# Linear attention before a GELU MLP on one core: 64-token blocks on 64x64 tiles, and groups of one chunk of each sequence

## The chip, the core and the metric

The kernel runs on one NeuronCore of a Trainium2 chip. Five engines work on their own queues, each strictly in the order of its instructions: TensorE (PE, matrix products, its weight loads shown as PEld), VectorE (DVE), ScalarE (ACT), GpSimd (POOL, which here also issues the loads) and SyncE (SP, which issues stores and transposing DMAs). They meet through semaphores. The metric is the device time of one execution in microseconds (us); lower is better.

## What is computed

Inputs q, k, v are 4 sequences x 8 heads x 768 tokens x 64 values; `lam` has one decay per head. Attention is causal and linear, with a decay of `lam` per token, and its result of 3072 tokens x 512 values goes through an MLP of width 2048 with an exact GELU. The reference, cut to what matters:

```python
for b in range(nb):                       # blocks of 64 tokens
    intra = einsum('bhic,bhjc->bhij', qb, kb) * Dmask     # lam ** (i - j), i >= j
    intra = einsum('bhij,bhjd->bhid', intra, vb)
    inter = einsum('bhid,bhde->bhie', qb * lam_pow, kv_state)
    out[:, :, sl] = intra + inter
    kv_state = lam_block * kv_state + einsum('bhsd,bhse->bhde', kb_dec, vb)
x = out as [B * S, H * D]
y = gelu(x @ w_in) @ w_out
```

The state is carried from block to block within a sequence, and sequences do not depend on each other.

## The kernel before, in words

Matrix operands are bf16, sums and results float32. The work is cut into 24 chunks of 128 tokens, numbered through sequence after sequence (six to a sequence), and into six groups of four consecutive chunks (`M = 4`). A group is 512 tokens, the width of one MLP pass. While PE runs the MLP of one group, the attention of the next is placed between the MLP's blocks.

The MLP of a group (`mlp_blocks`, L276) has 32 blocks: 16 of the first product (`mm1`, four matmuls of 512 columns, L288, then a GELU by ACT, L290) and 16 of the second (`mm2`, four matmuls of 512 columns, L300; after four blocks ACT copies the sum, L305, and SP stores it, L306).

The attention of a chunk has these steps:
- Loads of q, k and v, issued by POOL (L65), three or so chunks ahead (`prefetch`).
- `decay_k` (L157, L167): k times a decay per token, on POOL.
- Transposes of k and of q. The first eight chunks do it on PE (L174) with a copy by ACT (L180) and a product by DVE (L183, `qT`). From chunk 8 on, SP issues transposing DMAs (L189, L191), with `q_hat`, the scaled q, made by POOL in between (L190).
- `scores` (L193): eight matmuls on 64 rows x 128 columns (L198), each 128 columns long, into two banks of `sc`; DVE multiplies them by the mask (L202).
- `next_state` (L204): from chunk 4 on `next_state_full`, four matmuls over two heads each (L238), of which DVE keeps the diagonal blocks by a product with `lam_blk` (L245, L246). The first four chunks do it with eight matmuls of 64 columns on 128x64 tiles (L213). The last chunk of a sequence has no state to make.
- `outputs` (L249): the old state times q (L253, four matmuls; in the first four chunks L259, on 64x64 tiles; none in the first chunk of a sequence) and the masked scores times v (L263, eight matmuls on 128x64 tiles) into the one bank `o`. ACT (first eight chunks, L271) or DVE (L273) copies the result into x, transposed as the MLP wants it.

PE's order is written out by hand. Chunks 0 to 3 run ahead of the MLP (L371 to L396), with idle matmuls (`keep_warm`) between them. Chunks 4 to 7 are placed by the table `group0` into the MLP of group 0. From chunk 8 on, each step has a due time as a share of a group's MLP (`todo`, L438): transposes a third of a group ahead, scores and state of the i-th chunk at 0.06 + 0.245 i, its outputs at the time of the next chunk's scores. Steps that fall due together run in the order outputs, scores, state. PSUM has eight banks: two each for `mh`, `mo` and `sc`, one each for `o` and `t`.

Of the kernel before, what the change touches and what calls it, by code (L numbers as in the profile page):

```python
# [15 lines left out]
def kernel(  # L16
# [14 lines left out]
    C = 128  # L31
    NB = S // C
    NCH = B * NB
# [3 lines left out]
    assert NK1 == HP  # L37


    M = 4  # L40
    NG = NCH // M
    assert NG * M == NCH and M == 4 and NB == 6

# [4 lines left out]
    qkv_pool = ctx.enter_context(tc.tile_pool(name="qkv", bufs=8))  # L48
    work_pool = ctx.enter_context(tc.tile_pool(name="work", bufs=3))
# [4 lines left out]


# [3 lines left out]
    def chunk_of(name, n):  # L59
        b, so = n // NB, n % NB  # L60
        return dram[name][b, :, so * C:(so + 1) * C, :].rearrange("h si d -> si h d")

    def load(n, name):
        raw[n, name] = qkv_pool.tile([128, H, D], BF16, tag=name, name=f"{name}_t")
        nc.gpsimd.dma_start(raw[n, name], chunk_of(name, n))  # L65


    lam_b = consts.tile([128, H], F32)
    nc.sync.dma_start(lam_b, lam[None, :].to_broadcast((128, H)))

    pos = consts.tile([128, 1], F32)
    row = consts.tile([128, C], F32)
    nc.gpsimd.iota(pos, pattern=[[0, 1]], base=0, channel_multiplier=1, allow_small_or_imprecise_dtypes=True)
    nc.gpsimd.iota(row, pattern=[[1, C]], base=0, channel_multiplier=0, allow_small_or_imprecise_dtypes=True)

    for item in "k0 q0 v0 k1 q1 k2 q2 v1 k3 q3 v2 v3".split():
        load(int(item[1]), item[0])

    w_in_t = w_pool.tile([128, NK1, d_ff], BF16)
    w_out_t = w_pool.tile([128, NK2, d_model], BF16)  # L80
    w_in_r = moe_w_in.rearrange("(ko ki) f -> ki ko f", ki=128)
    w_out_r = moe_w_out.rearrange("(ko ki) f -> ki ko f", ki=128)
    NS = 4

    def load_w_in(s):
        f = d_ff // NS
        nc.gpsimd.dma_start(w_in_t[:, :, s * f:(s + 1) * f], w_in_r[:, :, s * f:(s + 1) * f])

    def load_w_out(s):
        f = NK2 // NS  # L90
        nc.gpsimd.dma_start(w_out_t[:, s * f:(s + 1) * f, :], w_out_r[:, s * f:(s + 1) * f, :])
# [4 lines left out]
    cmask = consts.tile([128, C], F32)  # L96
    negj = consts.tile([128, 1], F32)
    cmj = consts.tile([128, 1], F32)
    warm = consts.tile([128, 1], F32)
    nc.vector.tensor_scalar(ident, row, pos, None, op0=ALU.is_equal)  # L100
    nc.vector.tensor_scalar(cmask, row, pos, None, op0=ALU.is_ge)
    nc.vector.tensor_scalar(negj, pos, -1.0, None, op0=ALU.mult)
    nc.vector.tensor_scalar(cmj, pos, -1.0, float(C), op0=ALU.mult, op1=ALU.add)

    lam_blk = consts.tile([128, HP, 128], F32)
    first_blk = consts.tile([128, HP, 128], BF16)
    nc.vector.memset(lam_blk, 0.0)
    nc.vector.memset(first_blk, 0.0)


    ln = consts.tile([128, H], F32)
    ln_col = consts.tile([128, HP], F32)
# [3 lines left out]
    lam_k = consts.tile([128, H], F32)  # L116
    lam_c = consts.tile([128, HP], F32)
    dmask = consts.tile([128, H, C], F32)
    nc.scalar.activation(ln, lam_b, ACT.Ln)
    ln_r = ln.rearrange("p (hp hi) -> p hp hi", hi=2)  # L120
    for hi in range(2):
        p = slice(hi * D, (hi + 1) * D)
        nc.vector.tensor_copy(ln_col[p, :, None], ln_r[p, :, hi:hi + 1])
    nc.scalar.activation(lam_m, ln, ACT.Exp, scale=negj)
    for hp in range(HP):
        nc.scalar.activation(lam_q[:, hp, :], row, ACT.Exp, scale=ln_col[:, hp:hp + 1])
    nc.scalar.activation(lam_k, ln, ACT.Exp, scale=cmj)
    nc.scalar.activation(lam_c, ln_col, ACT.Exp, scale=float(C))
    nc.scalar.activation(lam_p, ln, ACT.Exp, scale=pos)
    lam_c_b = lam_c[:, :, None].to_broadcast((128, HP, D))  # L130

    def make_lam_blk():
        for hi in range(2):
            p = slice(hi * D, (hi + 1) * D)
            nc.vector.tensor_copy(lam_blk[p, :, p], lam_c_b[p])

    def make_dmask():
        nc.vector.tensor_mul(dmask, cmask[:, None, :].to_broadcast((128, H, C)),
                             lam_m[:, :, None].to_broadcast((128, H, C)))


# [3 lines left out]
    xT = {}  # L145
    states = {}

    def bank(shape, dtype, tag, name):
        return ps.tile(shape, dtype, tag=tag, name=name, bufs=2 if tag in ("sc", "mh", "mo") else 1)

    def begin(n, early=False):
        c = Chunk()
        c.n, c.sb, c.early = n, n % NB, early
        c.q, c.k, c.v = (raw.pop((n, name)) for name in "qkv")
        return c

    def decay_k(c, eng):  # L157

        if c.sb == NB - 1:
            return  # L160
        c.k_dec = work_pool.tile([128, H, D], BF16, tag="kd", name="k_dec")
        if eng is nc.scalar:
            for h in range(H):
                nc.scalar.activation(c.k_dec[:, h, :], c.k[:, h, :], ACT.Copy, scale=lam_k[:, h:h + 1])
        else:
            scale = lam_k if c.early else lam_m
            eng.tensor_mul(c.k_dec, c.k, scale[:, :, None].to_broadcast((128, H, D)))  # L167

    def transposes(c, between=lambda: None):

        t_ps = [bank([128, HP, C], BF16, tag, "t_ps") for tag in ("mh", "mo" if c.early else "mh")]
        for dst, src in zip(t_ps, (c.k, c.q)):
            for hp in range(HP):
                nc.tensor.transpose(dst[:, hp, :], src[:, 2 * hp:2 * hp + 2, :], ident)  # L174
            if src is c.k:
                between()
        c.kT = work_pool.tile([128, HP, C], BF16, tag="kT", name="kT")
        c.qT = work_pool.tile([128, HP, C], BF16, tag="qT", name="qT")
        if c.n > 0:
            nc.scalar.copy(c.kT, t_ps[0])  # L180
        else:
            nc.vector.tensor_copy(c.kT, t_ps[0])
        nc.vector.tensor_mul(c.qT, t_ps[1], lam_q)  # L183

    def dma_transposes(c):
        c.kT = work_pool.tile([128, HP, C], BF16, tag="kT", name="kT")
        c.qT = work_pool.tile([128, HP, C], BF16, tag="qT", name="qT")
# [5 lines left out]
    def scores(c):  # L193
        sc_ps = [bank([128, HP, C], F32, "sc", f"sc_ps{hi}") for hi in range(2)]
        for hp in range(HP):
            for hi in range(2):
                p = slice(hi * D, (hi + 1) * D)
                nc.tensor.matmul(sc_ps[hi][:, hp, :], c.kT[p, hp, :], c.qT[p, hp, :], start=True, stop=True)  # L198
        c.sc_m = work_pool.tile([128, HP, 2, C], BF16, tag="sc_m", name="sc_m")
        dmask_r = dmask.rearrange("p (hp hi) i -> p hp hi i", hi=2)  # L200
        for hi in range(2):
            nc.vector.tensor_mul(c.sc_m[:, :, hi, :], sc_ps[hi], dmask_r[:, :, hi, :])  # L202

    def next_state(c):  # L204
        if c.sb == NB - 1:
            return
        if not c.early:
            return next_state_full(c)
        kv_ps = bank([128, HP, D], F32, "t", "kv_ps")
        for hp in range(HP):  # L210
            for hi in range(2):
                h = 2 * hp + hi
                nc.tensor.matmul(kv_ps[hi * D:(hi + 1) * D, hp, :], c.k_dec[:, h, :], c.v[:, h, :],  # L213
                                 start=True, stop=True)
        if c.n == M - 1:
            for hi in range(2):
                p = slice(hi * D, (hi + 1) * D)
                nc.vector.tensor_add(first_blk[p, :, p], kv_ps[p], states[c.n][1][p])
            states[c.n + 1] = first_blk, None
            return  # L220
        new = work_pool.tile([128, HP, D], BF16, tag="state", name="state")
        if c.sb == 0:
            nc.vector.tensor_copy(new, kv_ps)
        else:
            nc.vector.tensor_add(new, kv_ps, states[c.n][1])
        old = work_pool.tile([128, HP, D], F32, tag="old", name="old")
        states[c.n + 1] = new, old

    def decay_state(c):
        new, old = states[c.n + 1]  # L230
        for hp in range(HP):
            nc.scalar.activation(old[:, hp, :], new[:, hp, :], ACT.Copy, scale=lam_c[:, hp:hp + 1])

    def next_state_full(c):

        kv_ps = bank([128, HP, 128], F32, "t", "kv_ps")
        for hp in range(HP):
            nc.tensor.matmul(kv_ps[:, hp, :], c.k_dec[:, 2 * hp:2 * hp + 2, :], c.v[:, 2 * hp:2 * hp + 2, :],  # L238
                             start=True, stop=True)
        new = work_pool.tile([128, HP, 128], BF16, tag="state_f", name="state")  # L240
        if c.sb == 0:
            nc.vector.tensor_mul(new, kv_ps, lam_blk)
        else:
            tmp = work_pool.tile([128, HP, 128], F32, tag="tmp", name="tmp")
            nc.vector.tensor_add(tmp, kv_ps, states[c.n][0])  # L245
            nc.vector.tensor_mul(new, tmp, lam_blk)  # L246
        states[c.n + 1] = new, None

    def outputs(c, x_t, off, evacuate=True):  # L249
# [16 lines left out]
        if evacuate:  # L266
            empty_outputs(c)
# [131 lines left out]
    for s in range(1, NS):  # L399
        load_w_in(s)  # L400
# [104 lines left out]
```

## Time and profile before

| what | us |
|---|---|
| median of three runs (lowest, highest) | 218.54 (217.63, 219.41) |
| span of the profiled execution, first to last instruction | 217.5 |
| median less that span | 1.04 |
| first MLP matmul starts | 19.37 |
| first matmul of the second product starts | 33.55 |
| MLP of group 1 starts | 54.05 |
| last copy of a result starts (chain) | 214.06 |

The profile comes from one execution. Of that execution the span is what is known; the runs' times were taken on their own, and the table sets their median beside it. A group of the profile is a line of the kernel, an engine, an operation and its tiles (out<-in), with the number of instructions, their busy time and the mean duration of one. A matmul's duration holds the way through the array; matmuls follow each other faster than that, so the pace is read from starts. A tile such as 64*128 is rows x columns of the array. The chain of work that ended last goes back from the last instruction to whatever released it.

Loads of q, k or v take POOL 0.88 to 0.92 us each to issue and, in the first 50 us, land 0.9 us apart; a quarter of w_in or w_out takes about 2.5 us more.

### The profile page before, as it was taken

The numbers are of one execution on the slowest core, as the hardware profiler recorded it, in microseconds if no ns is written. First come the engines' busy times: TensorE is split into PE (matmuls) and PEld (weight loads), VectorE is DVE, ScalarE is ACT, GpSimd is POOL, SyncE is SP. The second block draws the span as 40 slices with busy tenths as digits, with TensorE's granted clock in tenths as the row PEclk, the third lists the DMA queues.
The fourth block names the chain that finished last, engine by engine and source line by source line (L and its number), as shares of the span: only waits on it lengthen the run. The fifth ranks groups of instructions, "written<-read, shape, count | busy, mean of one in ns | idle before, by whom it ended". The sixth has DMA issues, their size and how long they took to land.

```text
span 217.5 us, 3545 instructions
## 1 busy us (share of the span) xinstructions
PE 204.9 (94%) x1422; PEld 102.9 (47%) x1446; DVE 74.8 (34%) x120; ACT 91.1 (42%) x169; POOL 105.8 (49%) x120
## 2 busy tenths in 40 slices
PE   7679999999987999999999999999999999999993
PEld 2355444555443544444545444544445545444452
DVE  5884000478516243316225323315415323100000
ACT  6975772434563321365221375221465221566121
POOL 8998333998999999276950809113000000000000
PEclk9999999999999999999999999999999999999998
DMA  5999999999999999999999497515251012100112
GB/s 37 149 169 203 198 194 183 156 208 148 177 150 126 164 128 138 215 110 104 109 114 160 77 180 62 37 48 146 74 98 24 3 57 88 50 0 3 48 49 96
DMA packets 100272, 24.35 MB, mean 112 GB/s; under 512 B 92960, under 2 KB 97312, under 8 KB 100256
## 3 DMA queue, kind: packets, MB, share of 16 engines
q0 software_dynamic: 79104, 13.64, 84.4%
q1 hardware_dynamic: 21152, 10.50, 22.7%
q8 instruction: 11, 0.18, 0.3%
q14 instruction: 5, 0.04, 0.1%
HBM read 27.27 MB, written 6.29 MB: 154 GB/s over the span
## 4 chain that ended last, share of the span: by engine, by line
PE 73%; DMA 14%; POOL 9%; issue 2%; ACT 0%; POOLq 0%
PE o_ps L300 33%; PE h_ps L288 28%; DMA q_t<-in_q_dram 8%; DMA qT<-q_hat 3%; DMA w_in_t<-in_moe_w_in_dram 3%; PE o_ps L263 3%; PE sc_ps L198 3%; POOL k_t L65 3%; POOL q_t L65 2%; POOL v_t L65 2%; PE kv_ps L238 2%; PE o_ps L315 2%; PE o_ps L253 2%; POOL k_dec L167 1%; POOL q_hat L190 1%
## 5 line engine op out<-in xcount | busy, mean ns | idle before, releaser
L288 PE MATMUL h_ps<-x_t,w_in_t 128*128 128x512 bf16 (+2 forms) x378 | 84.8, 377 | 1.0 <-DMA w_in_t<-in_moe_w_in_dram 0.5
L300 PE MATMUL o_ps<-w_out_t,g_t 128*128 128x512 bf16 x355 | 81.8, 379 | 0.8 <-issue 0.3
L290 ACT ACTIVATE g_t<-h_ps 128x512 bf16<-128x512 f32 x96 | 57.3, 597 | 35.3 <-PE h_ps L288 35.3
L288 PEld LDWEIGHTS <-w_in_t 128*128 128x128 bf16 x388 | 37.3, 98 | 43.8 <-DMA w_in_t<-in_moe_w_in_dram 0.6
L300 PEld LDWEIGHTS <-g_t 128*128 128x128 bf16 x368 | 34.7, 98 | 39.6
L305 ACT COPY o_sb<-o_ps 128x512 f32<-128x512 f32 x23 | 13.5, 586 | 68.3 <-PE o_ps L300 62.5
L202 DVE TENSOR_TENSOR sc_m<-sc_ps,dmask 128x512 bf16<-128x512 f32 x48 | 30.8, 683 | 16.1 <-PE sc_ps L198 15.8
L273 DVE CAST x_t<-o_ps 128x512 bf16<-128x512 f32 x16 | 11.1, 692 | 71.4 <-PE o_ps L263 71.4
L190 POOL TENSOR_TENSOR q_hat<-q_t,lam_p 128x512 bf16<-128x512 bf16 x16 | 16.9, 1056 | 20.0 <-DMA qT<-q_hat 19.0
L167 POOL TENSOR_TENSOR k_dec<-k_t,lam_m 128x512 bf16<-128x512 bf16 x16 | 17.7, 1106 | 14.0 <-PE kv_ps L238 8.1
L65 POOL DMA_DIRECT2D k_t<-in_k_dram x24 | 22.1, 920 | 4.0 <-DMA w_out_t<-in_moe_w_out_dram 2.1
L65 POOL DMA_DIRECT2D q_t<-in_q_dram x24 | 21.5, 897 | 4.2 <-DMA w_out_t<-in_moe_w_out_dram 3.4
L65 POOL DMA_DIRECT2D v_t<-in_v_dram x24 | 21.4, 894 | 3.4 <-DMA w_out_t<-in_moe_w_out_dram 1.7
L198 PE MATMUL sc_ps<-qT,kT 64*128 64x128 bf16 x192 | 9.5, 218 | 3.8 <-DMA qT<-q_hat 2.6
L246 DVE TENSOR_TENSOR state<-tmp,lam_blk 128x512 bf16<-128x512 f32 x13 | 12.1, 932 | 0.5
L183 DVE TENSOR_TENSOR qT<-t_ps,lam_q 128x512 bf16<-128x512 bf16 x8 | 5.5, 689 | 18.9 <-PE t_ps L174 18.7
L263 PE MATMUL o_ps<-sc_m,v_t 128*64 128x128 bf16 x192 | 10.1, 225 | 0.0
L198 PEld LDWEIGHTS <-kT 64*128 64x128 bf16 x192 | 5.7, 94 | 8.3 <-issue 4.7
L361 PE MATMUL idle_ps<-idle 128*128 128x512 bf16 x21 | 7.5, 473 | 1.2 <-DVE idle L94 1.2
L245 DVE TENSOR_TENSOR tmp<-kv_ps,state 128x512 f32<-128x512 f32 x12 | 8.2, 681 | 0.0
L180 ACT COPY kT<-t_ps 128x512 bf16<-128x512 bf16 x7 | 4.1, 579 | 9.4 <-PE t_ps L174 9.4
L263 PEld LDWEIGHTS <-v_t 128*64 128x64 bf16 x192 | 6.2, 109 | 3.3 <-issue 0.8
(57 smaller groups left out, 82.7 us busy)
## 6 DMA issues: line engine op xcount, KB each, us to landing
out_dram<-o_sb SPq DMA_DIRECT2D x23, 256.0 KB, 2.6
k_t<-in_k_dram POOLq DMA_DIRECT2D x24, 128.0 KB, 4.6
q_t<-in_q_dram POOLq DMA_DIRECT2D x24, 128.0 KB, 5.9
v_t<-in_v_dram POOLq DMA_DIRECT2D x24, 128.0 KB, 5.9
w_in_t<-in_moe_w_in_dram POOLq DMA_DIRECT2D x4, 512.0 KB, 7.9
w_out_t<-in_moe_w_out_dram POOLq DMA_DIRECT2D x4, 512.0 KB, 15.1
kT<-k_t SPq DMA_TRANSPOSE x16, 4.7
qT<-q_hat SPq DMA_TRANSPOSE x16, 4.0
```

The costliest lines, as they stand in the source:

```text
L65: nc.gpsimd.dma_start(raw[n, name], chunk_of(name, n))
L167: eng.tensor_mul(c.k_dec, c.k, scale[:, :, None].to_broadcast((128, H, D)))
L190: nc.gpsimd.tensor_mul(q_hat, c.q, lam_p[:, :, None].to_broadcast((128, H, D)))
L198: nc.tensor.matmul(sc_ps[hi][:, hp, :], c.kT[p, hp, :], c.qT[p, hp, :], start=True, stop=True)
L202: nc.vector.tensor_mul(c.sc_m[:, :, hi, :], sc_ps[hi], dmask_r[:, :, hi, :])
L246: nc.vector.tensor_mul(new, tmp, lam_blk)
L263: nc.tensor.matmul(o_ps[hi * D:(hi + 1) * D, hp, :], c.v[:, 2 * hp + hi, :], c.sc_m[:, hp, hi, :], start=(c.sb == 0 and hp == 0), stop=Tru ...
L273: nc.vector.tensor_copy(c.x_o, c.o_ps)
L288: nc.tensor.matmul(h_ps[:, lo:hi], w_in_t[:, ki, kf * 128:(kf + 1) * 128], x_t[:, ki, lo:hi], start=(ki == 0 and lo == 0), stop=(ki == NK1 ...
L290: nc.scalar.activation(g_t[:, kf, :], h_ps, ACT.Gelu)
L300: nc.tensor.matmul(om[io], g_t[:, kf, io * C:(io + 1) * C], w_out_t[:, kf, :], start=(kf == 0), stop=(kf == NK2 - 1))
L305: nc.scalar.copy(o_sb, om[io])
```

## The change

Groups are now one chunk of each of the four sequences, so the first group has no old state, and group g holds chunk g of every sequence. The result rows of a block are `io * S + g * C`.

Within a chunk, attention works in blocks of 64 tokens. All its matmuls from chunk 4 on are 64x64 tiles with 64 columns. Rows 0 to 63 of the array hold one head of a pair and rows 64 to 127 the other. Scores and states go to the columns of the same half, outputs to the other half (`half(1 - hi)`; w_in's rows are loaded swapped to match). `visit(f, d)` issues the outputs of chunk f and the scores and states of chunk d in turn, a pair of each. For this, v is loaded by block and head (`load_v`, four DMAs a group), k is copied into the same order (`by_block`, four copies, on ACT for chunks 4 to 7 and on DVE later), and v is decayed by POOL instead of k (`decay_v`). The state between the two blocks of a chunk is `mid`, copied by ACT except in the last group.

The first MLP pass starts with three chunks only: its first 10 blocks take 384 columns, and `rest` takes the fourth chunk's 128 columns later. Group 1 does so with its first 6 blocks. Chunk 3's attention, the first states and the table `dmask` come between MLP blocks. Placing is by block number: visits at blocks 3, 10, 17, 24 and 30 of a group, transposes (`prepare`) at 0, 7, 14 and 21; group 1 has its own list, moved by 2. The raw pools have ten buffers of q and k, the work pool four.

```diff
+    BANKS = dict(mh=2, mo=2, sc=2, o=1, kv=1)
+    def load_v(g):
+        t = raw[g] = qkv_pool.tile([128, 2, B * HP, D], BF16, tag="vg", name="vg_t", bufs=3)
+        src = v.rearrange("b (hp hi) s d -> hi s (b hp) d", hi=2)
+        for u in range(2):
+            for hi in range(2):
+                s = g * C + u * L
+                nc.gpsimd.dma_start(t[half(hi), u], src[hi, s:s + L])
+    for hi in range(2):
+        nc.sync.dma_start(lam_h[half(hi)], lam_pair[hi:hi + 1, :].to_broadcast((64, HP)))
     nc.sync.dma_start(lam_b, lam[None, :].to_broadcast((128, H)))
...
+    def load_w_in(lo, hi_):
+        f = slice(lo * 128, hi_ * 128)
+        for hi in range(2):
+            nc.gpsimd.dma_start(w_in_t[half(1 - hi), :, f], w_in_r[hi, :, :, f])
+    for n in range(3):
+        for name in "kqv":
+            load(n, name)
+    load_w_in(0, 2)
+    load_w_in(2, 5)
+    load_w_in(5, 8)
+    for name in "kqv":
+        load(3, name)
+    load_w_in(8, 12)
+    load_w_in(12, 16)
+    for s in range(4):
+        load_w_out(4 * s, 4 * s + 4)
...
+    def by_block(c, eng):
+        c.k2 = work_pool.tile([128, 2, HP, D], BF16, tag="k2", name="k2")
+        k_r = c.k.rearrange("p (hp hi) d -> p hp hi d", hi=2)
+        for hi in range(2):
+            for u in range(2):
+                if eng is nc.scalar:
+                    nc.scalar.copy(c.k2[half(hi), u], k_r[half(u), :, hi, :])
+                else:
+                    eng.tensor_copy(c.k2[half(hi), u], k_r[half(u), :, hi, :])
+    def decay_v(n):
+        vd[n] = work_pool.tile([128, 2, HP, D], BF16, tag="vd", name="vd", bufs=6)
+        nc.gpsimd.tensor_mul(vd[n], v_of(n), lam_vb)
     def scores(c):
+        sc = c.sc = bank([128, 2, HP, L], F32, "sc", "sc_ps")
+        return [[(sc[half(hi), u, hp, :], c.kT[half(hi), hp, u * L:(u + 1) * L],
+                  c.qT[half(hi), hp, u * L:(u + 1) * L], True) for hi in range(2)]
+                for u in range(2) for hp in range(HP)]
+    def states(c):
+        kv = c.kv = bank([128, 2, HP, D], F32, "kv", "kv_ps")
+        us = range(2) if c.g < NG - 1 else range(1)
+        return [[(kv[half(hi), u, hp, :], c.k2[half(hi), u, hp, :], vd[c.n][half(hi), u, hp, :], True)
+                 for hi in range(2)] for u in us for hp in range(HP)]
+    def next_states(c):
...
+        if c.g == NG - 1:
+            nc.vector.tensor_add(c.mid, c.kv[:, 0], s0)
+            return
+        nc.vector.tensor_add(t1, c.kv[:, 0], s0)
+        nc.scalar.copy(c.mid, t1)
+        nc.vector.tensor_add(t2, c.kv[:, 1], t1)
...
+        nc.vector.tensor_mul(new, t2, lam_cb)
+    def outputs(c):
...
+        for u, s in enumerate((state[c.n], c.mid)):
+            for hp in range(HP):
+                pairs.append([(o[half(1 - hi), hp, u * L:(u + 1) * L], s[half(hi), hp, :],
+                               c.qT[half(hi), hp, u * L:(u + 1) * L], False) for hi in range(2)])
+        for u in range(2):
+            for hp in range(HP):
+                pairs.append([(o[half(1 - hi), hp, u * L:(u + 1) * L], c.v[half(hi), u, hp, :],
+                               c.sm[half(hi), u, hp, :], False) for hi in range(2)])
...
+    def visit(f, d, emptier=None):
...
+        if d:
+            kv = states(d)
+            lists.append(scores(d) + kv)
+        if f:
+            lists.append(outputs(f))
+        issue(*lists)
+        if f:
+            empty(f, emptier or nc.vector)
+        if d:
+            mask(d)
+            next_states(d)
...
+    def prepare(n):
+        c = begin(n)
+        dma_transposes(c)
+        decay_v(n)
+        by_block(c, nc.vector)
+        prefetch(n + B)
+    prefetch(2 * B - 1)
+    for n in range(B, 2 * B):
+        decay_v(n)
+    prefetch(2 * B + 1)
+    ahead = {
+        5: [lambda: pe_transposes(begin(3), ("mo", "mo"))],
+        6: [lambda: scores0(3)],
+        8: [lambda: outputs0(3, nc.scalar)],
+        9: [make_dmask, lambda: decay_k0(0, nc.vector)],
...
+        first: [first_states],
+        first + 8: [group1(4)],
+        first + 11: [lambda: visit(None, 4)],
+        first + 12: [group1(5)],
+        first + 13: [lambda: visit(4, 5, nc.scalar)],
+        first + 14: [group1(6)],
+        first + 15: [lambda: visit(5, 6, nc.scalar)],
+    }
...
+    visit(6, None, nc.scalar)
+    plans = {1: (2, 8, 9, 14, 15, 20, 21, 26, 27, 31)}
+        if g == 1:
+            ahead[1] += [group1(7)]
+            ahead[3] += [lambda: visit(None, 7)]
+            ahead[5] += [lambda: visit(7, None, nc.vector)]
...
+            p = plans.get(g, (None, 3, 0, 10, 7, 17, 14, 24, 21, 30))
```

`first` is 19, the block after the first product of group 0. `scores0`, `outputs0` and `first_states` do the four chunks of group 0, which need no old state, with tiles of 128 tokens as before. `group1(n)` is the PE transposition of a chunk with `by_block` on ACT. `issue` walks through its lists and takes one pair of each in turn.

## The prediction

> **What bounds the kernel now.** I read the page's busy shares first, then the slices of the span, then the chain of work that ended last, and then the timelines of single engines around one attention visit.
>
> ```profile
> PE 204.9 (94%) x1422; PEld 102.9 (47%) x1446; DVE 74.8 (34%) x120; ACT 91.1 (42%) x169; POOL 105.8 (49%) x120
> ...
> DMA  5999999999999999999999497515251012100112
> ...
> PE 73%; DMA 14%; POOL 9%; issue 2%; ACT 0%; POOLq 0%
> ```
>
> TensorE (PE) is busy for 94% of the span, and from 66.57 us on the chain runs on it alone; the DMA engines are full over the first 22 of 40 slices. So PE decides, except where a load or a transpose is late. The MLP is 768 matmuls of 512 columns at 0.216 us, about 166 us, and the change leaves it. What can shrink is the attention between its blocks and the stretch ahead of them. The chain, in order of time (start, length, what), prices one attention visit; the PE timeline shows small tiles:
>
> ```profile
> 106.53 0.22 PE o_ps L253 x4
> 106.75 0.34 PE o_ps L263 x8
> 107.10 0.33 PE sc_ps L198 x8
> 107.43 0.33 PE kv_ps L238 x4
> ```
>
> ```profile
> 15.19 0.32 PE L213 MATMUL kv_ps<-v_t,k_dec 128*64 128x64 bf16 x8
> ...
> 18.04 0.41 PE L259 MATMUL o_ps<-qT,state 64*64 64x128 bf16 x8
> ```
>
> A full visit costs 1.22 us. Of that, L253 runs at 0.055 us a matmul of 128 columns; L263 and L198 take 0.34 and 0.33 for four pairs at about 0.056, so each holds about 0.1 us for the switch between tile shapes, and so does L238. L213 puts eight 64-column matmuls into 0.32 us though one lasts 0.20: their starts spread over 0.12 us, a pair per 0.03 us, two column tiles at a time. L259 is the one 64x64 row: eight matmuls of 128 columns in 0.41 with 0.216 for one, so a pair per 0.055 to 0.06, two tiles at a time on the diagonal. Four tiles at a time occur nowhere.
>
> **Steady visits (chunks 8 to 23).** Before: 16 x 1.22, less three without a state (0.33 each) and two without an old state (0.22 each), 18.1 us; the four places where the chain shows 0.97 for four MLP matmuls instead of 0.86 add 0.4: 18.5. After: 64 matmuls of 64 columns, 32 pairs, of which a diagonal pair (scores, states) stands beside an off-diagonal one (outputs). If four tiles run at once, 16 steps of 0.03, 0.46 us, plus 0.19 for the switch in and out: 0.65. The first and the last visit of a group have 16 pairs alone: 0.65 too. Five visits in each of four groups: 13.0. Gain 5.5. The bounds: pairs strictly in turn make a full visit 1.12, all matmuls singly 2.05. I take four at once, since L213 shows two streams down one set of rows, L198 two row tiles writing the same partitions of two banks, and a step needs nothing else.
>
> Two rules of the Trainium skill speak against it. TensorE: Matmul & The Clock Gate ("Wait — 56ns, not 53.3ns?") has starts never closer than about 25 ns; L213's are closer, but only sixteen instructions long. By that rule an estimate for a full visit is 64 x 25 ns, 1.6 us, and the whole some 20 us slower. TensorEngine Tiling (Array Packing), "Gotcha 1: PSUM Pressure", says that row tiles cannot use one PSUM bank at the same time; L259's two row tiles share o_ps and still pair. By that rule the visit would be the 1.12 case.
>
> **Chunks 4 to 7.** Before, from the chain between 39.17 and 53: transposes 4 x 0.45, scores 4 x 0.33, states 0.77, old states 3 x 0.22, outputs 4 x 0.34, and 0.3 of switches: 6.2. After: the same transposes, 1.8, and six visits of 0.65: 5.7. Gain 0.5.
>
> **Start.** Loads land 0.9 us apart from 6.65 on. Before, h_ps starts at 19.37, behind twelve loads and a quarter of w_in. After, nine loads end near 13.3 and the first slice of w_in (half a quarter; a quarter takes 2.5 us) near 14.6. Chunk 2's queries land near 12.4; then qT 0.69, scores 0.33, two masks 1.3, outputs 0.34, ACT copy 0.59 bring h_ps to about 16.1. The two extra lam loads on SP (0.39 us of issue, as lam_b) delay tables by 0.8, which the DVE's queue absorbs to 0.3. But chunk 3 (1.1 us with switches) and the first states (2 x 0.24 and switches, 0.65) now lie behind 16.1, its queries land near 20.1 (0.5 wait), and w_in's fourth piece near 23.5 (0.2 wait). The second product starts at 16.1 + 13.9 + 1.1 + 0.65 + 0.9 = 32.7, against 33.55. Gain 0.9; bounds 2 and -0.5.
>
> **Waits the change adds around chunks 4 to 7.** Each of by_block's four ACT copies is 64x256; nearest rows are L319 (128x256, 0.37) and L164 (128x64, 0.25 apart), so 0.41 each. After a transposition at t, kT is copied from t+0.47 (as 42.44 to 42.91), the copies end at t+2.65, and the visit one block later wants its first state at t+1.65. PE is in order, so the rest of the visit and the next MLP block queue behind it: 0.9 each for chunks 5 and 6. Chunk 4 waits for vd on POOL: vg's four loads land near 42.2, decay_v takes 1.1, PE comes near 43: 0.3. The next group's first block needs chunk 6's x, an ACT copy (0.59 and its start) with no block between: 0.7. Chunk 7's transposes share mh with the first product: 0.7. A late mid: 0.1. Together 3.6, against 0.2 of small gaps before: loss 3.4. Bounds 0 and 5.
>
> **A wait on ACT.** mid is copied by ACT, in its queue ahead of the next gelu. These rows show the order and pace:
>
> ```profile
> 99.08 0.69 DVE L273 CAST x_t<-o_ps 128x512 bf16<-128x512 f32 x1 [5.77 <-PE o_ps L263]
> 99.68 1.28 DVE L202 TENSOR_TENSOR sc_m<-sc_ps,dmask 128x512 bf16<-128x512 f32 x2
> ```
>
> ```profile
> 98.66 0.60 ACT L290 ACTIVATE g_t<-h_ps 128x512 bf16<-128x512 f32 x1 [0.27 <-PE h_ps L288]
> 100.52 0.60 ACT L290 ACTIVATE g_t<-h_ps 128x512 bf16<-128x512 f32 x1 [1.27 <-PE h_ps L288]
> ```
>
> A gelu starts 1.06 us after its block (99.46 to 100.52) and ends at 1.66; PE wants that bank back at 1.73. After the change: DVE starts 0.18 into the block, x 0.60, mask 0.60, t1 0.41 (L225), ACT 0.05 and 0.40: gelu starts at 2.24, 1.1 too late for PE two blocks on. Without x (a group's first visit) 0.5. Visits at blocks 3 and 10 lie in the first product in groups 2 and 3 (chunks of the last group copy mid on DVE), and one half visit in group 1: 2 x 1.6 + 0.5 = 3.7 lost. Visits in the second product have no gelu behind them. Bounds 0 (ACT idles 0.27 a block) and 5.
>
> **POOL and the transposes.** The kernel before already waits for qT, as the list of waits has it:
>
> ```profile
> PE sc_ps L198 <- DMA qT<-q_hat: 2.6, 2, 2.2
> ```
>
> POOL is busy almost without a break from 38 to 86. The ten w_in loads instead of four cost it 6 x 0.8 more, in the stretch from 20 to 38 where it sat idle 11 us in all before L65, waiting for landings; vg's four loads have as many short rows as four of v. After: four decay_v end near 46.5, eight loads at 0.88 near 53.5, q_hat and decay_v of chunk 8 near 55.6, then ten loads (prefetch to 12, with vg of group 3) to 64.8, and only then q_hat of chunk 9, which ends near 65.9. Its transposition lands 4.0 later (median), 6.9 at worst, near 70; PE comes near 68.6. Wait 1.5 instead of 2.6: gain 1.1; bounds 2.6 gain and 3 loss. SP has only its finished stores ahead. Later chunks have two loads between them and 12 blocks of time.
>
> **Costed at nothing.** DVE's by_block, four copies of at most 0.29 (L135) a chunk: DVE is busy 11.5 of 33 us a group, and the next visit is ten blocks off. Without that cover, 1.2 us a chunk. (An SBUF operation of DVE, L246, stretches from 0.69 to 1.83 while POOL works; even so it fits.) decay_v replaces k_dec at the same 1.1. The split first products reload 64 weight tiles: at 0.003 each beyond the columns, 0.2 lost.
>
> **Sum:** -5.5 - 0.5 - 0.9 + 3.4 + 3.7 - 1.1 + 0.2 = -0.7. The profiled execution spans 217.5; that becomes 216.8. The median of the three runs, 218.54, is 1.04 above that span, which I add for what lies around it: 217.8.
>
> **Rivals.**
> Pairs in turn. For it: no row with four tiles at once, and 128 PE instructions in 0.46 us, twice the density of L213. Against: nothing in L213, L198 or L259 collides. Fourteen full visits take 0.46 longer each, the last three 0.12 less than that: +6.1, 223.9. It decides from 0.2 us a visit on (14 x 0.2 = 2.8 us, over 1%).
> Waits smaller. If ACT's wait and half of those around chunks 4 to 7 are hidden (gelu's bank free earlier, copies shorter), 217.8 - 3.7 - 1.7 = 212.4. For it: DVE and ACT are idle half the time. Against: both queues are in order, and PE's slack is 0.07.
> Transposes late. If q_hat of chunk 9 lands behind ten loads as 59.67 did (6.9 us) and the next two follow suit: +4, 221.8. For it: DMA is full until 114. Against: old chunk 9 had the same and lost 2.2.
>
> **How the numbers follow.** One per cent is about what a measurement can tell: 216.4 to 220.7. Forecast 0.42, own range 215.5 to 220.5 (faster 0.09, same 0.30, slower 0.03). Pairs in turn 0.20, slower. Waits smaller 0.25, faster. Transposes late 0.13, slower 0.11, same 0.02. So faster 0.34, same 0.32, slower 0.34. The range for 8 in 10 reaches into the cases on both sides: 212.4 to 223.9.
>
> **What would show it.** Matmuls of a full visit within about 0.5 us, or 0.9 and more; idle PE of about 1 us two blocks after the visits at blocks 3 and 10 of groups 2 and 3, released by gelu, with ACT's gelu behind mid; PE waiting for the ACT copies of k2 around 45 to 52; the first h_ps near 16; one wait for qT near 69. If a visit takes over 0.85 us, or PE waits elsewhere by more than 3 us, the forecast is wrong.

## The result and the profile after

The changed kernel takes 232.99 us, median of 4 runs (232.14 to 233.70), against 218.73 for the kernel before on the same chip: ratio 1.0666, 95% interval 1.0615 to 1.0716. It is slower by 14.3 us, outside the range of 212.4 to 223.9. The profiled execution spans 231.1 us and took 232.84 by its own time. The time lies about 1.75 us above the span in this and the experiments' runs, where the prediction had added 1.04. Executions more than 1.5% above the fastest of their kernel are left out of what follows unless the text says so: two of four of the kernel without the two loads (230.3 and 231.9), four of eight of the one with whole rows (221.2 to 221.7, not profiled), three single ones of later kernels (720.5, 1157.2 and 219.9), and some of the kernel before.

The page of the changed kernel, in the order in which the lines of before were read:

```profile
PE 203.9 (88%) x2250; PEld 104.1 (45%) x2279; DVE 98.2 (42%) x189; ACT 97.5 (42%) x187; POOL 109.1 (47%) x128
...
PEclk9679999999999999889999999999999999999999
DMA  0999999998999999999999325103234011200112
...
PE 69%; DMA 13%; POOL 6%; ACT 4%; issue 2%; DVE 2%; SPq 1%; POOLq 0%; ACTq 0%
```

PE is busy 1.0 us less than before (204.9), in a span 13.6 us longer: nearly everything that was lost is idle PE. The first of 40 slices of the DMA line has fallen from 5 to 0, and PEclk, before at 9 up to its last slice, shows two dips, in slices 2 and 3 and in slices 17 and 18. DVE, SP's queue and, with more than 0%, ACT have entered the chain.

To place the loss, the starts of each group's MLP are read from PE's timeline (us):

| stretch | before | after | after less before |
|---|---|---|---|
| start to the second product of group 0 | 33.55 | 41.06 | +7.5 |
| from there to the MLP of group 1 | 20.5 | 20.8 | +0.3 |
| group 1 | 35.1 | 41.6 | +6.5 |
| group 2 | 32.4 | 32.65 | +0.25 |
| group 3 | 32.2 | 32.65 | +0.45 |
| group 4 | 32.4 | 31.2 | -1.2 |
| group 5 to the end of the span | 31.3 | 31.1 | -0.2 |

Two stretches hold all of it. What PE waited for (engine, tile and line, releaser: total us, times, longest), from the list of PE's waits after; it covers the whole span, and its row with `g_t` L346 belongs to groups 2 and 3:

```profile
PE t_ps L187 <- DMA k_t<-in_k_dram: 5.9, 1, 5.9
PE sc_ps L279 <- DMA qT<-q_hat: 4.1, 2, 3.4
PE h_ps L344 <- ACT x_t L269: 2.1, 3, 0.8
PE h_ps L344 <- ACT g_t L346: 2.0, 2, 1.0
...
PE h_ps L354 <- DVE x_t L271: 0.9, 1, 0.9
PE sc_ps L279 <- ACT k L209: 0.8, 1, 0.8
```

**The start.** The DMA part of the profile, for the first 12 us alone (40 slices of 0.3 us; under it the packets of SP's queue, and issues with their number, size and median us to landing), of the kernel before and then of the changed one:

```profile
DMA  0000000000249996899999999999999999999999
q1 hardware_dynamic: 144, 0.00, 0.5%
k_t<-in_k_dram POOLq DMA_DIRECT2D x4, 128.0 KB, 4.4
```

```profile
DMA  0000000000000000000000039996999999999999
q1 hardware_dynamic: 688, 0.01, 3.1%
k_t<-in_k_dram POOLq DMA_DIRECT2D x3, 128.0 KB, 9.4
lam_h<-in_lam_dram SPq DMA_DIRECT2D x2, 1.0 KB, 6.2
```

POOL issues its first load at the same time in both (1.38 and 1.39), but its packets start to flow at 3.14 before and at 6.99 after. Ahead of them, SP's queue has 544 packets more: the two `lam_h` loads take every second value of a row, so each of their 512 values is a piece of 4 bytes. They land at 5.80 and 8.90, `lam_b` at 10.55 instead of 3.29, and chunk 0's keys at 10.72 instead of 5.06, which is the wait of 5.9. At 7.79, 2.9 into this wait, the clock drops to half, and it comes back at 14.62. The first line below is that stretch, the second one the dip in group 1; the columns are the stretch, busy time (instructions) of PE, PEld, DVE, ACT and POOL, the granted clock, the DMA share and GB/s:

```profile
7.80:14.60 6.80, 3.17 (x13) 1.52 (x14) 2.08 (x3) 3.98 (x13) 3.53 (x5) 0.50 2.09 133
96.50:99.90 3.40, 3.40 (x9) 1.19 (x8) 3.26 (x9) 0.99 (x2) 3.38 (x5) 0.51 2.16 169
```

**The transposes of group 1.** The second dip follows the longest wait of the second stretch. The chain of work (start, length, what) around it, and one row of POOL's timeline:

```profile
85.92 0.59 ACT o_sb L365
...
86.53 0.33 SPq L366
...
86.97 1.23 SPq L198
...
88.36 6.82 DMA qT<-q_hat
...
95.23 0.22 PE sc_ps L279 x2
...
96.09 4.01 PE o_ps L373 x10
```

```profile
81.10 1.06 POOL L199 TENSOR_TENSOR q_hat<-q_t,lam_p 128x512 bf16<-128x512 bf16 x1
```

SP issues in order. The store of block 21's result (L366) stands ahead of chunk 11's two transposes and waits for ACT's copy, which waits for PE. SP's last issue before it, chunk 10's second transposition, ended at 79.54; it then issues nothing until the store at 86.53. So chunk 11's transposes, whose `q_hat` (the fourth of the group on POOL, the row above) was finished at 82.16, are issued at 86.97 and 88.36. The second lands 6.82 later, and PE has waited 3.42 us for it. Issued at 82.2 and with the same 6.82, it would have landed at about 89.0, before PE came at 91.81 (an estimate from these rows). Then the clock is 0.51 for 3.4 us: the last line has ten MLP matmuls in 4.01 us instead of 2.16.

**The visits.** PE's timeline of the first full visit of group 1:

```profile
79.89 0.22 PE L279 MATMUL sc_ps<-qT,kT 64*64 64x64 bf16 x2 [0.70 <-DMA qT<-q_hat]
79.90 0.22 PE L279 MATMUL o_ps<-qT,state 64*64 64x64 bf16 x2
79.92 0.22 PE L279 MATMUL sc_ps<-qT,kT 64*64 64x64 bf16 x2
79.95 0.20 PE L279 MATMUL o_ps<-qT,state 64*64 64x64 bf16 x2
...
80.38 0.21 PE L279 MATMUL kv_ps<-vd,k 64*64 64x64 bf16 x2
80.39 0.20 PE L279 MATMUL o_ps<-sm,vg_t 64*64 64x64 bf16 x2
80.53 0.82 PE L344 MATMUL h_ps<-x_t,w_in_t 128*128 128x512 bf16 x2
```

Each line is a pair, a pair of each kind starts every 0.03 us, and the visit takes 0.64 us (79.89 to 80.53), where the rows of before make 1.22.

**The wait on ACT.** The chain in group 2, two blocks behind the visit at block 10:

```profile
113.91 0.69 DVE x_t L271
...
114.63 0.69 DVE sm L231
115.32 0.34 DVE t L246
...
115.69 0.41 ACT mid L247
116.09 0.51 ACT g_t L346
...
116.64 1.46 PE h_ps L344 x6
```

These are the copies that the prediction named, in its order; PE loses 1.0 us here, and the same in group 3 (the 2.0 in the list of waits). At the half visits of block 3 there is no such wait.

### The profile page after: what moved, and what is told of

Read it like the earlier page. It is cut to its first block, busy times and chain, and to the rows that moved or that the text cites. A ratio compares the mean times of both kernels' runs of the same rounds, so it can differ in the third digit from the quotient of the medians.

```text
span 231.1 us, 5286 instructions
## 1 busy us (share of the span) xinstructions
PE 203.9 (88%) x2250; PEld 104.1 (45%) x2279; DVE 98.2 (42%) x189; ACT 97.5 (42%) x187; POOL 109.1 (47%) x128
## 4 chain that ended last, share of the span: by engine, by line
PE 69%; DMA 13%; POOL 6%; ACT 4%; issue 2%; DVE 2%; SPq 1%; POOLq 0%; ACTq 0%
PE o_ps L373 31%; PE h_ps L344 28%; DMA q_t<-in_q_dram 8%; DMA qT<-q_hat 5%; PE sc_ps L279 3%; POOL k_t L72 2%; PE o_ps L279 2%; PE kv_ps L279 2%; POOL q_t L72 2%; PE o_ps L384 2%; POOL vg_t L81 1%; ACT k L209 1%; DVE sm L231 1%; ACT g_t L346 1%; PE h_ps L354 1%
## 5 line engine op out<-in xcount | busy, mean ns | idle before, releaser
L344 PE MATMUL h_ps<-x_t,w_in_t 128*128 128x512 bf16 (+1 forms) x373 | 83.5, 370 | 5.2 <-ACT x_t L269 2.1
L373 PE MATMUL o_ps<-w_out_t,g_t 128*128 128x512 bf16 x351 | 82.2, 385 | 2.0 <-issue 1.7
L346 ACT ACTIVATE g_t<-h_ps 128x512 bf16<-128x512 f32 (+1 forms) x96 | 55.0, 579 | 28.7 <-PE h_ps L344 28.3
L365 ACT COPY o_sb<-o_ps 128x512 f32<-128x512 f32 (+1 forms) x25 | 14.2, 569 | 55.7 <-PE o_ps L373 50.2
L211 DVE COPY k<-k_t 64x256 bf16<-64x256 bf16 x64 | 31.3, 489 | 0.8
L220 POOL TENSOR_TENSOR vd<-vg_t,lam_v 128x512 bf16<-128x512 bf16 x20 | 21.0, 1056 | 2.9 <-DMA vg_t<-in_v_dram 2.9
L231 DVE TENSOR_TENSOR sm<-sc_ps,dmask 128x512 bf16<-128x512 f32 x20 | 13.8, 691 | 16.3 <-PE sc_ps L279 14.9
L81 POOL DMA_DIRECT2D vg_t<-in_v_dram x20 | 16.4, 842 | 3.8 <-DMA w_out_t<-in_moe_w_out_dram 3.0
L279 PE MATMUL sc_ps<-qT,kT 64*64 64x64 bf16 (+1 forms) x352 | 10.4, 197 | 6.5 <-DMA qT<-q_hat 4.1
L251 DVE TENSOR_TENSOR state<-t,lam_c 128x256 bf16<-128x256 f32 x16 | 11.4, 712 | 0.6
L279 PE MATMUL o_ps<-sm,vg_t 64*64 64x64 bf16 x320 | 8.7, 194 | 0.0
```

What stands on the lines that cost most here:

```text
L81: nc.gpsimd.dma_start(t[half(hi), u], src[hi, s:s + L])
L211: eng.tensor_copy(c.k2[half(hi), u], k_r[half(u), :, hi, :])
L220: nc.gpsimd.tensor_mul(vd[n], v_of(n), lam_vb)
L231: nc.vector.tensor_mul(c.sm, c.sc, dmask)
L279: nc.tensor.matmul(out_, lhsT, rhs, start=start, stop=True, skip_group_check=True)
L344: nc.tensor.matmul(h_ps[:, :hi], w_in_t[:, ki, kf * 128:(kf + 1) * 128], x_t[:, ki, :hi], start=(ki == 0), stop=(ki == NK1 - 1))
```

## The experiments

The theory after the result: the four tiles work as forecast, and the loss is (a) the two `lam_h` loads, (b) transposes placed too late in group 1, with the half clock behind the wait, (c) ACT's `mid`. The rival for (a): two more DMAs on SP, whatever their pieces, or w_in's ten loads. The rival for (b): DMA is too full at that time, and an earlier issue only waits longer.

**The two loads alone, in the kernel before.** Their result is not used.

```diff
+    lam_h = consts.tile([128, HP], F32)
+    lam_pair = lam.rearrange("(hp hi) -> hi hp", hi=2)
+    for hi in range(2):
+        nc.sync.dma_start(lam_h[hi * 64:(hi + 1) * 64], lam_pair[hi:hi + 1, :].to_broadcast((64, HP)))
     nc.sync.dma_start(lam_b, lam[None, :].to_broadcast((128, H)))
```

> The kernel before with the two lam_h loads ahead of lam_b, whose result nothing reads. Theory: its loads too begin 5 to 6 us later, 218.7 becomes about 224 to 225. Rival (it takes the new order of loads): within 1 of 218.7, apart from up to 1 us of later lam_b.

Measured: 224.53 against 218.0, ratio 1.0294 [1.0227, 1.0362]. The first 12 us of the DMA part and the longest of PE's waits repeat the changed kernel's:

```profile
DMA  0000000000000000000000059996999999999999
q1 hardware_dynamic: 688, 0.01, 3.0%
```

```profile
PE t_ps L178 <- DMA k_t<-in_k_dram: 6.3, 1, 6.3
```

The clock falls to half here too (0.53 between 7.8 and 14.6), and once more between 17.59 and 24.42, so the 6.2 us are not the late landing alone.

**The same two DMAs with whole rows.** As above, but each loads 64 rows of eight contiguous values, 128 pieces of 32 bytes.

```diff
+    for hi in range(2):
+        nc.sync.dma_start(lam_w[hi * 64:(hi + 1) * 64], lam[None, :].to_broadcast((64, H)))
```

> The kernel before with two more loads to 64 partitions each ahead of lam_b, but in pieces of 8 contiguous floats (128 pieces in all, not 512 of one float); nothing reads them. Theory (the number of small pieces counts): first load late by 1 us or less, time within 1.5 of 218.7. Rival (any two more DMAs on SP ahead of the loads do it): late by 4 us or more, 223 or more.

Measured, in the four executions counted: ratio 1.0001 [0.9945, 1.0058]; POOL's first packets flow at 3.15, and chunk 0's keys land at 5.93.

```profile
DMA  0000000000394989999999999999999999999999
q1 hardware_dynamic: 304, 0.01, 1.6%
```

So it is the cutting into 512 pieces of 4 bytes, not two more DMAs. Whether the number of the pieces or their size counts, and what exactly they hold up between SP's queue and POOL's, was not tried.

**The changed kernel without the two loads.** `ln_h` comes from `ln` (all heads on every partition) by two small DVE copies.

```diff
-    for hi in range(2):
-        nc.sync.dma_start(lam_h[half(hi)], lam_pair[hi:hi + 1, :].to_broadcast((64, HP)))
...
-    nc.scalar.activation(ln_h, lam_h, ACT.Ln)
+    ln_r = ln.rearrange("p (hp hi) -> p hp hi", hi=2)
+    for hi in range(2):
+        nc.vector.tensor_copy(ln_h[half(hi), :, None], ln_r[half(hi), :, hi:hi + 1])
```

> The changed kernel with ln_h made from ln by two DVE copies, as the kernel before does, in place of the two lam_h loads. Theory (the 64x4 loads of single floats hold up every load of POOL): k of chunk 0 lands near 5.1 instead of 10.7, the second product starts near 35.5 instead of 41.1, the half clock between 7.8 and 14.6 goes, and the time falls from 233.0 by 5 to 6 to about 227.5. Rival (the new order and the ten w_in pieces delay the loads): k of chunk 0 lands near 10 as now, time within 1 of 233.

Measured: 226.2 and 228.2, in the mean 1.042 of the 218.0 of the kernel before (after: 1.0666), and 5.8 us below the changed kernel. The ratio on record is 1.0510 [1.0415, 1.0605]; it fits the median of all four executions, 229.2. In the profile, of the execution of 226.2, chunk 0's keys land at 5.11, the first h_ps starts at 16.10, where the prediction had 16.1, and the second product at 34.85 instead of 41.06. In the other four profiles with this start (four experiments further down) the second product starts at 34.4 to 35.6. The forecast was 32.7: the difference is in waits for chunk 3's keys and queries, `qT` and w_in behind the first h_ps. The wait for `qT` in group 1 is still there (3.2), with half the clock behind it.

**Earlier transposes in group 1 alone.** In the changed kernel, `prepare` of chunks 8 to 12 at blocks 2, 6, 11, 17 and 24 instead of 4, 11, 17, 23 and 29; visits as they were.

```diff
-    plans = {1: (2, 8, 9, 14, 15, 20, 21, 26, 27, 31)}
+    plans = {1: (0, 8, 4, 14, 9, 20, 15, 26, 22, 31)}
```

> The changed kernel with the transposes of chunks 8 to 12 issued 2 to 6 blocks earlier in group 1 (blocks 2, 6, 11, 17, 24 instead of 4, 11, 17, 23, 29), so that none stands on SP behind the store after block 21. Theory (the transposes are issued too late): the waits for qT of 0.7 and 3.4 and the half clock after them go, time falls by 4 to 6 to about 228. Rival (POOL's ten loads ahead of q_hat and the full DMA engines make qT late wherever it is issued): the waits stay within 1 us of 4.1 in sum, time within 1.5 of 233.

Measured: 228.31, ratio 1.0485 [1.0409, 1.0562]. Group 1 takes 37.2 instead of 41.6, and the half pace behind the wait is gone: the 19 MLP matmuls behind chunk 11's visit take 4.26, where the changed kernel's took 5.95. (The pace says so, not the clock row: this profile shows a clock of 1.00 throughout, although its first four transposes take 0.61 as in the changed kernel, whose row shows 0.50 there.) Of the two waits for `qT` one of 1.0 is left:

```profile
PE sc_ps L279 <- DMA qT<-q_hat: 1.0, 1, 1.0
```

The edit both takes the transposes away from behind the store and gives them up to six blocks more, so by itself it does not tell the two apart; that the place behind the store is enough to make chunk 11's wait is the estimate from the rows above. What is left of the rival is a landing of 6.6 us behind the 1.0, which is chunk 9's. A new gap of 0.9 ahead of a matmul of the states (at 87.08) came with the earlier plan; the profile names no releaser for it.

**Both edits.**

> Both edits together: ln_h computed from ln, and the earlier transposes in group 1. Theory (the two losses are separate): the gains add, 233.0 - 5.7 - 4.7 = about 222.6, with no half clock left. Rival (loads that start earlier leave the transposes early enough anyway, or both collide on the same DMA engines): no more than the better of the two alone, 226 to 228.

Measured: 220.15 (219.83 to 220.86), ratio 1.0100 [1.0044, 1.0156]. By the ratios the two edits take off 12.4 us (0.0566 of 218.6) of the 14.3. The theory's sum of the two gains, about 222.6, was too high by 2.4: group 1 takes 34.9 here against 37.2 with the plan alone, and the waits of 1.0 and 0.9 left there are gone, so the losses were not separate. The second product starts at 35.04, groups 2 and 3 still take 32.65 each, and the wait on ACT is the only one listed in them (PE's waits from 88 us on):

```profile
PE h_ps L342 <- ACT g_t L344: 2.0, 2, 1.0
```

**`mid` on VectorE too.** DVE makes `mid` directly from the kv bank, by a second addition, ahead of `t1`.

```diff
+        nc.vector.tensor_add(c.mid, c.kv[:, 0], s0)
         nc.vector.tensor_add(t1, c.kv[:, 0], s0)
-        nc.scalar.copy(c.mid, t1)
```

> As the run with both edits, and mid is made by a second DVE addition from the state bank, not copied by ACT. Theory (ACT's wait for mid holds the next gelu, 1.15 us twice): 2.3 below the run with both edits, about 220.3, and no gap of 1.1 us two blocks after the visits at block 10 of groups 2 and 3. Rival (the time of that wait comes back elsewhere, DVE being longer by 0.4 a visit): within 0.7 of the run with both edits.

Measured: about 218.1, ratio 1.0000 [0.9964, 1.0035]. The waits on GELU two blocks behind the visits are gone, and groups 2, 3 and 4 take 31.3, 31.3 and 31.2, against 32.4, 32.2 and 32.4 before. Without its two large misses the change is no faster than the kernel before: in these profiles 3.2 us are won in the three groups, while the second product of group 0 starts 2.0 later, the stretch behind it is 0.4 and group 1 1.1 longer. (The profiled execution took 219.54, 1.4 above the median: it has a wait of 2.2 for chunk 3's queries, and a gap of 1.0 in group 1 for which the profile names no releaser.)

**Pairs in turn.** As the last kernel, but a visit issues all of one list and then the other.

```diff
-        for i in range(max(map(len, lists))):
-            for pairs in lists:
-                if i < len(pairs):
...
+        for pairs in lists:
+            for pair in pairs:
...
```

> As the run with all three edits, but a visit issues its lists one after the other (scores and states, then outputs), so that only two tiles stand side by side. Theory (four tiles run at once when issued in turn): a full visit takes 1.1 us instead of 0.64, fourteen of them, 6 us above the run with all three edits. Rival (the array's tiles overlap by themselves or the order does not matter): within 1 us of it.

Measured: 222.50, ratio 1.0209 [1.0153, 1.0265], 4.4 over the interleaved one. A visit (PE's timeline, runs of one tile put together) takes 101.56 to 102.59, 1.03 us:

```profile
101.56 0.44 PE L276 MATMUL sc_ps<-qT,kT 64*64 64x64 bf16 x16
101.83 0.32 PE L276 MATMUL kv_ps<-vd,k 64*64 64x64 bf16 x10
101.97 0.22 PE L276 MATMUL o_ps<-qT,state 64*64 64x64 bf16 x2
...
102.59 0.60 PE L341 MATMUL h_ps<-x_t,w_in_t 128*128 128x512 bf16 x2
```

Groups 2 to 4 take 32.5, 32.5 and 32.0, about as in the kernel before: the gain of the steady groups is the interleaving. It costs less than the 6.1 of the rival. A visit is 0.39 longer, not 0.47: the outputs' first matmuls start while the states' list still runs (lines two and three). Of the 4.4, 3.2 lie in groups 2 to 4; the rest is not told apart from the start, which differs by 1.2 between the two profiles.

**More of the waits around chunks 4 to 7.** On the kernel with all three edits: k2 of chunks 4 to 7 half by ACT and half by DVE, their visits a block earlier, chunk 7's transposes in the `mo` banks, seven split blocks in group 1.

```diff
-        first + 8: [group1(4)],
-        first + 11: [lambda: visit(None, 4)],
+        first + 7: [group1(4)],
+        first + 10: [lambda: visit(None, 4)],
...
-                if eng is nc.scalar:
+                if eng is None and hi == 0:
                     nc.scalar.copy(c.k2[half(hi), u], k_r[half(u), :, hi, :])
```

> As the run with all three edits, and four waits around chunks 4 to 7 taken away: k2 of these chunks is copied half by ACT and half by DVE, the five visits come one block earlier so that an MLP block lies between the last one and the next group, chunk 7's PE transposes use the banks of mo, and group 1 holds back its fourth chunk for 7 blocks instead of 6. Theory (each wait is PE's own): 1.6 + 0.8 + 0.7 + 0.8, 3.9 below the run with all three edits, about 216.4, below the kernel before. Rival (chunk 4's loads or the next late thing take the place): within 1.5 of the run with all three edits.

Measured: about 218.3, ratio 0.9995 [0.9954, 1.0037], no gain. The waits moved: between 36 and 62 us PE now waits 0.9 for `qT` from DVE, 0.8 for `mid` and 0.3 for k2.

**The start reordered, on the kernel with all three edits and on the one just above.** The loads of w_in's columns 8 and 9 ahead of chunk 3's values; chunk 3's keys transposed ahead of block 6, its queries ahead of block 7, scores at 8, outputs at 10, the table and the first decays two blocks later.

```diff
-    for name in "kqv":
-        load(3, name)
-    load_w_in(8, 12)
-    load_w_in(12, 16)
+    load(3, "k")
+    load(3, "q")
+    load_w_in(8, 10)
+    load(3, "v")
+    load_w_in(10, 13)
+    load_w_in(13, 16)
```

> The kernel with all three edits (lam table from lam_b, earlier plan, mid on VectorE), and the start reordered: the loads of chunk 3's keys and queries stay ahead of w_in's columns 8 to 9, its values come behind them, its transposes lie one and two blocks later (keys ahead of block 6, queries ahead of block 7), its scores at 8, its outputs at 10. Theory (the start lost its advantage because chunk 3's loads and w_in come just too late for the places they have): the waits for k, q and qT of chunk 3 and for w_in, 2.4 to 3.3 us together, shrink to about 1.2, the second product of group 0 starts near 33.0 instead of 35.0 to 35.6, the time falls by about 2 to 216.2, about 1% below the kernel before. Rival (the stretch is limited by the bytes to be loaded, whatever their order): the second product stays at 34.5 or later, the wait is put down to w_in or to x of chunk 3, and the time stays within 0.8 of 218.1.

> The same reordered start on the variant that also has visits of chunks 4 to 6 one block earlier and k2 copied half by ScalarE, half by VectorE. Theory: second product near 33.0 instead of 35.3, the time about 2 below 218.2. Rival: second product at 34.5 or later, time unchanged within 0.8, or the gain is given back in waits for loads of chunks 4 to 7, whose loads do not come earlier (the second group's first product then still starts near 55.5).

Measured, with 217.7 for the kernel before: 218.08, ratio 1.0005 [0.9979, 1.0032], and 217.74, ratio 0.9997 [0.9962, 1.0033]. No gain is shown, though the start does move: the second product begins at 33.63 and 34.21 instead of 34.4 to 35.6, the second of them hardly beyond that spread. In the first of the two, group 1 gives it back with a wait for one transposition behind loads of k:

```profile
PE sc_ps L288 <- DMA qT<-q_hat: 1.8, 1, 1.8
```

No version was found that beats the kernel before by more than these intervals.

## Why the prediction was wrong

Its mechanism for the visits was right; it failed on two terms, the start and the transposes, whose causes it had not seen.

- **Steady visits, -5.5.** Right in the visit, a little too large in sum. A full visit takes 0.64 (forecast 0.65). Groups 2 to 4 win 0.9 to 1.25 each once nothing else is in them (forecast about 1.4), and pairs in turn, the first rival, lose all of it. The Trainium skill, TensorE: Matmul & The Clock Gate ("Wait — 56ns, not 53.3ns?"), says that starts never come closer than about 25 ns; here 64 matmuls start within 0.50 us, some 8 ns apart, over four tiles. Its page TensorEngine Tiling (Array Packing), "Gotcha 1: PSUM Pressure", was the other objection; row tiles that share a bank ran side by side all the same. The measurement decides in both.
- **Start, -0.9.** This step failed first: it measured +7.5. The sentence "The two extra lam loads on SP (0.39 us of issue, as lam_b) delay tables by 0.8, which the DVE's queue absorbs to 0.3" priced the loads by their issue and asked only who needs their data. What counted was the 512 pieces of 4 bytes, and that POOL's loads wait for them: by the experiment that removes them, 6.2 of the 7.5. The Trainium skill states in DMA: Bandwidth & Descriptors, "Rules for kernel authors", that a strided last dimension becomes one descriptor (one piece for a DMA engine to move) per element; the packet counts (688 against 144, 512 of the difference being the values) agree, and the prediction passed it over. The other 1.3, and 2.15 against the forecast of 32.7, are waits behind the first h_ps: the prediction had allowed 0.9 there (it names 0.5 and 0.2 of it), and in that experiment PE's starts before chunk 3's keys, queries and scores, before w_in's columns, x and GELU's banks fall behind its pace by 3.0 in all. The profile counts 1.9 of that as idle; the rest was not told apart. With the earlier transposes the first h_ps came 1.4 later than in the changed kernel (23.70) and the second product at about the same time (41.11), the waits in between being 1.2 shorter: an earlier first h_ps alone is not an earlier second product.
- **POOL and the transposes, -1.1.** This step failed second. The waits for `qT` are 4.1 against 2.6 before, and the half clock costs another 1.7: +3.2. "SP has only its finished stores ahead" was false: a store not yet finished, block 21's, stood ahead of chunk 11's transposes. The wait that the term did price, 1.5 for chunk 9 behind POOL's ten loads, measured 0.7. The rival "transposes late" (0.13) expected late transposes, but from those loads, with no store in the way and no price for the clock: that its +4 on the forecast lies near the 4.3 by which this term was off is luck. Group 1's plan gives its transposes five or six blocks, the other groups' mostly ten; the prediction had counted 12 for the later chunks.
- **Waits around chunks 4 to 7, +3.4.** About right in sum: 0.8 and 0.3 on ACT's k2 copies, 0.7 on chunk 6's x, 0.9 on x by DVE, 0.4 for chunk 7's bank, 3.1 together. The 0.9 on x by DVE was not forecast; the copies were forecast at 0.9 each, and chunk 4's wait for the decayed v did not come.
- **ACT's `mid`, +3.7.** Right in place, too large: 1.0 in two places by the waits, 2.0 in all by the last edit's time. The 0.5 behind half visits was not there.
- **Chunks 4 to 7, -0.5, and split products, +0.2.** Not told apart from the terms around them.
- **Costed at nothing.** The copies of `by_block` on DVE stayed hidden, though not by their length. Their group (mean ns of one after the busy time) has 31.3 us instead of the 18.6 that 64 at 0.29 would make. The median of one is 224 ns, the longest 2583; all 21 above 300 ns lie beside work of POOL (15 short ones do too), and the 16 after 150 us, where POOL is done, take at most 226.

```profile
L211 DVE COPY k<-k_t 64x256 bf16<-64x256 bf16 x64 | 31.3, 489 | 0.8
```

With both failed steps mended the time is 220.15, 2.3 above the forecast; 0.7 of that is the time outside the span.

## What to carry to other kernels

Price a small load by the pieces that it is cut into and by which loads of other queues come behind it, not by its issue time or by who needs its data. Give a transposing DMA its lead from the last unfinished store ahead of it in the same queue, with the longest landing seen and not the median, and add the clock that a long wait costs: here waits of 3.2 and 3.4 us were each followed by 3.41 us at half clock (1.7 us lost), a wait of 2.2 in the kernel before by none. A saving of 1 us a group can be real and still lose to one late load at the start: place the new work's waits before summing its gains.

## What the runs showed of the hardware

- Two loads on SP of 256 pieces of 4 bytes each delay POOL's loads issued beside them: first packets 6.99 instead of 3.14, first landing 5.7 us later. With 64 pieces of 32 bytes each the first packets come at 3.15 and the first landing 0.9 later, and the executions counted take the same time as without them.
- Sixty-four matmuls of 64 columns on four 64x64 tiles start within 0.50 us, and the visit takes 0.64 with its switches; two lists after one another take 1.03.
- PE idle for 3.42 us up to 95.23 was followed by half the clock from 96.54 to 99.95; without the two loads, 3.23 up to 88.38 by half the clock from 89.78 to 93.19. In the idle of 5.90 us at the start (4.86 to 10.77) it fell at 7.79 and came back at 14.62, 3.85 after work resumed.
- A clock row can miss a drop: with the earlier transposes it shows 1.00 from 7.8 to 14.6, while four transposes take 0.61 there, as at the 0.50 that the changed kernel's row shows.
